# Round 0 sums its exponentials on VectorE, and v loads in three transfers per pair of heads

## The chip, the cores and the metric

One NeuronCore of a Trainium2 chip runs the whole program. The metric is device time in microseconds, the median of several runs. The engines named here are PE (TensorE, matrix products), DVE (VectorE), ACT (ScalarE), POOL (GpSimd) and SP (SyncE, which here only issues transfers).

## The reference

The program is an attention with capped scores, followed by a gated feed-forward block. There are 4 batch elements, 12 heads, 448 tokens and 64 features per head; the block has 768 inputs and 1536 inner features.

```python
def _attn_ref(q, k, v, cap):                       # q, k, v: (4, 12, 448, 64)
    scores = 1.0 / np.sqrt(64) * np.matmul(q, k.transpose(0, 1, 3, 2))
    scores = cap * np.tanh(scores / cap)
    attn = np.exp(scores - np.max(scores, axis=-1, keepdims=True))
    attn = attn / (np.sum(attn, axis=-1, keepdims=True) + 1e-09)
    return np.matmul(attn, v)

def _moe_ref(x, w_gate, w_val, w_out, rms_g):      # x: (1792, 768)
    xn = x / np.sqrt(np.mean(x * x, axis=-1, keepdims=True) + 1e-06) * rms_g
    g = xn @ w_gate                                # (768, 1536)
    return g * (1.0 / (1.0 + np.exp(-g))) * (xn @ w_val) @ w_out
```

The weights w_gate, w_val and w_out arrive as 64-bit floats.

## The kernel before

**Attention.** A round (`duo`, L397) handles two pairs of heads, a and b, so four heads; there are three rounds per batch element, twelve in all. Pair p of batch element b has the slot 6b + p, and slots take turns in two raw buffers (`raw0`, `raw1`), four transposed buffers (`qk0` to `qk3`) and four v buffers (`v0` to `v3`). Each pair loads q and k in eight transfers (`load_qk`, L365) and v in four (`load_v`, L377); DVE transposes raw into qk (`turn_qk`, L387).

A round has seven units. Each of the first six takes 128 keys of one pair: score products on PE into a wide bank, a tanh and an exp on ACT (128 x 896 elements each) into one of four buffers `e`, and the product with v on PE. The seventh unit takes the last 64 keys of both pairs. The sum of the exponentials over the keys is made in one of two ways. In rounds 0 to 7 PE multiplies every `e` by a matrix of ones into bank 6, after units 1, 3, 5 and 6. In rounds 8 to 11 (`SUM_FIRST`, L392) DVE first adds the six wide `e` of each pair, and PE then sums over partitions once. At the end of a round DVE transposes bank 6, inverts it, transposes that and scales the products in their banks into `xT`; ACT squares `xT`.

**Between attention and block** (`xconv`, L495) PE sums the squares over all heads into bank 6, DVE transposes that (`sumsq<-bank`), makes the inverse root, and scales six tiles of `xT`; ACT and DVE split each into two 16-bit parts, `xhl`.

**Block.** `ffn1` (L531) is 24 groups of 18 products of 128 x 448 columns per batch element, `out_proj` (L550) the second product. The weights are turned from 64-bit to 32-bit floats by DVE (`to_f32`, L284) and split into 16-bit parts by ACT and DVE: w_gate and w_val of batch 0 in `conv_gv` (L312), w_out in `conv_out` and `split_out`. Their staging buffers hold four pairs of tiles of 768 KB (four loads lead, L601; later ones wait for a buffer).

**Order.** Every operation is put into a list with a due time; `Plan.schedule` (L82) goes through the engines with assumed costs and takes, of the operations that are ready, the one due first. The result is a fixed order on each engine, and each engine works in that order. The due times of the block hang on `F0`, `L0`, `L1` (L253): batch 0's block is due from F0 on. Attention of batch 0 is due from 14 on, 2.15 per unit, and that of batch 1 from 70 on.

Of the kernel before, what the change touches and what calls it, by code (L numbers as in the profile page):

```python
# [10 lines left out]
F32 = mybir.dt.float32  # L11
# [7 lines left out]
P = 128  # L19
B, H, S, D = 4, 12, 448, 64  # L20
NPAIR = H // 2
NDUO = H // 4
# [108 lines left out]
def capped_attention__then__swiglu_ffn(  # L131
# [20 lines left out]
    V, A, G, T, SP = nc.vector, nc.scalar, nc.gpsimd, nc.tensor, nc.sync  # L152
# [9 lines left out]
    def free(ap):  # L162
        n = 1
        for x in ap.shape[1:]:
            n *= x
        return n

    def op(e, name, due, dst, *args, cost=None, **kw):
        reads = [x for x in (*args, *kw.values()) if isinstance(x, bass.AP)]
        writes = [dst]  # L170
        if "accum_out" in kw:
            writes.append(kw["accum_out"])
            reads = [x for x in reads if x is not kw["accum_out"]]
        n = free(dst) / 1000
        if cost is None:
            if e is A:
                cost = 0.2 + n * 0.92 + (0.19 if "accum_out" in kw else 0.0)
            elif e is V:
                quick = name in ("tensor_scalar", "tensor_copy", "tensor_single_scalar")
                quick = quick and all(x.space != PSUM for x in reads)  # L180
                cost = 0.16 + n * (0.54 if quick else 1.07)
            else:
                cost = 0.25 + n * 2.3
        plan.add(str(e.engine), cost, due, lambda: getattr(e, name)(dst, *args, **kw), writes, reads)  # L184
# [10 lines left out]
    def dma(due, dst, src, e=None):  # L195
        size = free(dst) * dst.shape[0] * mybir.dt.size(dst.dtype)
        q = e or SP
        plan.add("SP" if q is SP else str(q.engine), 0.52, due, lambda: q.dma_start(dst, src), [dst], [src], moved=size)  # L198
# [23 lines left out]
    cu = const.tile([P, DM], F32, name="cu")  # L222
# [3 lines left out]
    hT = const.tile([P, 2, NF, S], F16, name="hT")  # L226
# [23 lines left out]
    OUT_STAGE = (4, 5, 6, 7, 4, 5, 7, 4, 6, 5, 7, 6)  # L250


    F0, L0, L1 = 82.0, 178.0, 165.0  # L253
    start_of = [F0, F0 + L0, F0 + L0 + L1, F0 + L0 + 2 * L1]
    length = [L0, L1, L1, 124.0]
    ATT = ((70.0, 3.0), (135.0, 5.0), (250.0, 5.0))
# [4 lines left out]
    def att_due(b, d, step):  # L261

        n = 7 * d + step
        if b == 0:
            return 14.0 + 2.15 * n
        s, step = ATT[b - 1]
        return s + n * step
# [91 lines left out]
    def slot(b, p):  # L359
        return b * NPAIR + p  # L360

    def x_slot(b, p):
        return slot(b, p) % (NPAIR + 2)
# [13 lines left out]
    def load_v(b, p, due):  # L377

        t = v_t[slot(b, p) % 4]
        for hh in range(2):  # L380
            src = v[b, 2 * p + hh]
            dma(due, t[:, 3 * hh : 3 * hh + 3], src[0:384].rearrange("(c j) d -> j c d", c=3))
            dma(due, t[HALF[(hh + p) % 2], 6], src[384:S])

    HALF = (slice(0, 64), slice(64, 128))

    def turn_qk(b, p, due):  # L387
        raw, t = raws[slot(b, p) % 2], qk_t[slot(b, p) % 4]
        op(V, "transpose", due, t, raw)

    units = [0]
    SUM_FIRST = 8  # L392
    old_w = wo_all[:, 8 * DM : 10 * DM]
    acc_wide = old_w[:, 0 : 2 * S].rearrange("p (h s) -> p h s", h=2)
    acc = [[acc_wide[:, 0], acc_wide[:, 1]], [old_w[:, 2 * S : 3 * S], cu[:, 0:S]]]

    def duo(b, d):  # L397
        pa, pb = 2 * d, 2 * d + 1
        for p in (pa, pb):
            due = att_due(b, d, 0.5 * (p - pa))  # L400
            load_qk(b, p, due - 20)
            load_v(b, p, due - 12)
            turn_qk(b, p, due - 6)
        total = bank[6][:, 0:S]
        pv = [bank[i][:, 0:S] for i in ((4, 5) if b == 0 else (0, 1))]
        vt = [v_t[slot(b, p) % 4] for p in (pa, pb)]
        qk = [qk_t[slot(b, p) % 4] for p in (pa, pb)]
        es = {}
        for n in range(7):
            due = att_due(b, d, n)  # L410
            wide = pair[units[0] % 2 if b == 0 else 1]
            e = es[n] = e_t[units[0] % 4]
            units[0] += 1
            x, c = n % 2, n // 2
            if n < 6:
                mm(due, 0.9, *[
                    (wide[:, hh, 0:S], qk[x][HALF[hh], 1, c * P : (c + 1) * P], qk[x][HALF[hh], 0], True, True)
                    for hh in range(2)
                ])
            else:  # L420
                mm(due, 0.9, *[
                    (wide[HALF[(hh + x) % 2], x, 0:S], qk[x][HALF[hh], 1, 384:S], qk[x][HALF[hh], 0], True, True)
                    for x in range(2) for hh in range(2)
                ])
            op(A, "activation", due, e, wide[:, :, 0:S], AF.Tanh, scale=sc_t)
            op(A, "activation", due, e, e, AF.Exp, scale=capt)
            if n < 6:
                mm(due + 3, 0.85, *[
                    (pv[x][HALF[hh]], vt[x][:, 3 * hh + c], e[:, hh], c == 0, False) for hh in range(2)
                ])  # L430
            else:
                mm(due + 3, 0.85, *[
                    (pv[x][HALF[hh]], vt[x][HALF[(hh + x) % 2], 6], e[HALF[(hh + x) % 2], x], False, True)
                    for x in range(2) for hh in range(2)
                ])
            if NDUO * b + d >= SUM_FIRST:
                if n in (2, 3, 4, 5):
                    old = es[x] if n < 4 else None
                    if x == 0:
                        op(V, "tensor_add", due + 3, acc_wide, acc_wide if old is None else old, e)  # L440
                    else:
                        for hh in range(2):
                            op(V, "tensor_add", due + 3, acc[1][hh], acc[1][hh] if old is None else old[:, hh], e[:, hh])
                elif n == 6:
                    for y in range(2):
                        for hh in range(2):
                            h = HALF[(hh + y) % 2]
                            op(V, "tensor_add", due + 3, acc[y][hh][h], acc[y][hh][h], e[h, y])
                    mm(due + 4, 0.9, *[
                        (total[32 * (2 * hh + y) : 32 * (2 * hh + y) + 32], ones[:, 0:32], acc[y][hh], True, True)  # L450
                        for y in range(2) for hh in range(2)
                    ])
                continue
            if x == 1:
                mm(due + 4, 0.85, *[
                    (total[32 * (2 * hh + y) : 32 * (2 * hh + y) + 32], ones[:, 0:32], es[n - 1 + y][:, hh], c == 0, False)
                    for y in range(2) for hh in range(2)
                ])
            if n == 6:
                mm(due + 4, 0.85, *[  # L460
                    (
                        total[32 * (2 * hh + y) : 32 * (2 * hh + y) + 32],
                        ones[HALF[(hh + y) % 2], 0:32], e[HALF[(hh + y) % 2], y], False, True,
                    )
                    for y in range(2) for hh in range(2)
                ])
        due = att_due(b, d, 7) + 3
        xp = x_slot(b, pa)
        tmp = xT[:, xp]
        op(V, "transpose", due, tmp, total)  # L470
        first = tmp.rearrange("p (n i) -> p n i", i=32)[:, :, 0]
        op(V, "reciprocal", due, inv_t, first.unsqueeze(1).to_broadcast([P, 2, R14]), cost=0.3)
        for x in range(2):
            inv = inv_t[:, x]
            for hh in range(2):
                r = 64 * hh + 32 * x
                o = 64 * hh + 32 * (1 - x)
                op(V, "reciprocal", due, inv[o : o + 32], first[r : r + 32], cost=0.25)
        op(V, "transpose", due, dn_t, inv_t.unsqueeze(3).to_broadcast([P, 2, R14, 32]))
        both = xT[:, xp : xp + 2]  # L480
        if b == 0:
            for x in range(2):
                op(V, "tensor_mul", due, xT[:, xp + x], pv[x], dn_t[:, x])
        else:
            op(V, "tensor_mul", due, both, pair[0][:, :, 0:S], dn_t)
        if d == 0:
            op(A, "activation", due + 1, sumsq, both, AF.Square)
        else:
            op(A, "activation", due + 1, dn_t, both, AF.Square)
            if d < NDUO - 1:  # L490
                op(V, "tensor_add", due + 1, sumsq, sumsq, dn_t)
# [107 lines left out]
    for d in range(NDUO):  # L599
        duo(0, d)  # L600
# [51 lines left out]
```

## Time and profile before

| What | us |
|---|---|
| median of 3 runs (lowest, highest) | 731.34 (730.57, 732.25) |
| the profiled execution | 731.7 |
| its span, first to last instruction | 729.9 |
| PE busy in the span | 702.6 (96%) |
| DVE, ACT busy | 374.3, 331.3 |

The profile is one execution; 1.8 us of its time lie outside its span. Times below are from the start of the span. PE's busy time is the union of its products, so the rest, 27.3 us, is time in which PE had none.

### The profile page before, as it was taken

The numbers are of one execution on the slowest core, as the hardware profiler recorded it, in microseconds if no ns is written. First come the engines' busy times: TensorE is split into PE (matmuls) and PEld (weight loads), VectorE is DVE, ScalarE is ACT, GpSimd is POOL, SyncE is SP. The second block draws the span as 40 slices with busy tenths as digits, with TensorE's granted clock in tenths as the row PEclk, the third lists the DMA queues.
The fourth block names the chain that finished last, engine by engine and source line by source line (L and its number), as shares of the span: only waits on it lengthen the run. The fifth ranks groups of instructions, "written<-read, shape, count | busy, mean of one in ns | idle before, by whom it ended". The sixth has DMA issues, their size and how long they took to land.

```text
span 729.9 us, 9854 instructions
## 1 busy us (share of the span) xinstructions
PE 702.6 (96%) x3956; PEld 315.8 (43%) x3956; DVE 374.3 (51%) x606; ACT 331.3 (45%) x450; POOL 12.9 (2%) x18
## 2 busy tenths in 40 slices
PE   5987799999999899999999999999999999999998
PEld 1222233333443244443455553345555655555564
DVE  1667788888889894625223219762222162222211
ACT  5888777878568883344511105721111121111100
POOL 0001000100000000000000000000000000000000
PEclk9999899999999989999999999999999999999999
DMA  8895686845644514400000010000000100000010
GB/s 178 177 230 102 151 221 170 201 126 169 180 142 152 111 24 90 86 13 22 4 1 1 1 33 12 22 12 1 1 0 1 33 34 12 1 1 0 6 39 33
DMA packets 137741, 50.98 MB, mean 70 GB/s; under 512 B 114144, under 2 KB 136160, under 8 KB 137696
## 3 DMA queue, kind: packets, MB, share of 16 engines
q1 hardware_dynamic: 133984, 49.90, 27.0%
q10 hardware_dynamic: 3712, 0.46, 0.4%
q8 instruction: 31, 0.51, 0.3%
q14 instruction: 14, 0.11, 0.1%
HBM read 44.83 MB, written 5.51 MB: 69 GB/s over the span
## 4 chain that ended last, share of the span: by engine, by line
PE 86%; DMA 4%; DVE 4%; SPq 4%; ACT 1%; issue 1%; DVEq 0%
PE bank L191 71%; PE banks L191 15%; SPq L198 4%; DMA raw<-in_q_dram 2%; DVE wslot L184 1%; DVE cu L184 1%; DVE wo_all L184 1%; DMA wo_all<-in_moe_w_val_dram 1%; DMA osb_t<-in_moe_w_val_dram 1%; DMA osb_t<-in_moe_w_gate_dram 1%; ACT e L184 1%; DMA raw<-in_k_dram 1%; DVE qk L184 0%; ACT osb_t L184 0%; DVE xT L184 0%
## 5 line engine op out<-in xcount | busy, mean ns | idle before, releaser
L191 PE MATMUL bank<-xhl,wslot 128*128 128x448 f16 x1728 | 336.1, 353 | 0.5 <-DVE t L184 0.5
L191 PEld LDWEIGHTS <-wslot 128*128 128x128 f16 x1728 | 165.3, 98 | 183.9 <-issue 33.6
L184 DVE SCALAR_TENSOR_TENSOR t<-t,bank 128x448 f32<-128x448 f32 x96 | 59.5, 620 | 161.7 <-ACT t L184 83.5
L191 PEld LDWEIGHTS <-hT 128*128 128x128 f16 (+1 forms) x1152 | 97.5, 101 | 85.9 <-issue 28.8
L191 PE MATMUL bank<-wo_all,hT 128*128 128x384 f16 (+1 forms) x768 | 126.5, 327 | 0.0
L184 ACT ACTIVATE e<-banks,sc_t 128x896 f32<-128x896 f32 x84 | 84.0, 1001 | 45.3 <-PE banks L191 43.9
L191 PE MATMUL banks<-qk 64*128 64x448 f32 (+1 forms) x384 | 87.7, 597 | 14.8 <-DVE qk L184 10.5
L184 ACT ACTIVATE e<-e,capt 128x896 f32<-128x896 f32 x84 | 87.5, 1041 | 2.5
L184 ACT ACTIVATE hT<-t 128x448 f16<-128x448 f32 x48 | 27.6, 574 | 121.1 <-DVE t L184 121.1
L184 ACT ACTIVATE t<-bank,hs 128x448 f32<-128x448 f32 x48 | 30.4, 633 | 94.9 <-PE bank L191 94.8
L191 PE MATMUL bank<-osb_t,hT 128*128 128x384 f16 (+1 forms) x384 | 72.2, 337 | 0.0
L184 ACT ACTIVATE wo_all<-bank,sm 128x384 f32<-128x384 f32 x28 | 16.2, 580 | 107.5 <-PE bank L191 107.5
L184 DVE SCALAR_TENSOR_TENSOR wo_all<-bank,sm,wo_all 128x384 f32<-128x384 f32 x28 | 17.2, 614 | 92.0 <-PE bank L191 87.7
L191 PE MATMUL banks<-e,v 128*64 128x448 f32 (+1 forms) x288 | 60.2, 567 | 0.8 <-ACT e L184 0.8
L191 PEld LDWEIGHTS banks<-qk 64*128 64x128 f32 (+1 forms) x384 | 25.5, 177 | 63.1 <-issue 27.7
L184 DVE SCALAR_TENSOR_TENSOR hT<-hT,t 128x448 f16<-128x448 f16 x48 | 29.8, 622 | 26.3 <-ACT hT L184 26.2
L191 PE MATMUL bank<-e,ones 128*32 128x448 f32 (+1 forms) x256 | 31.7, 571 | 4.9 <-DVE sumsq L184 4.9
L184 DVE STREAM_TRANSPOSE qk<-raw 128x896 f32<-128x896 f32 x24 | 26.2, 1102 | 18.5 <-DMA raw<-in_q_dram 12.1
L191 PEld LDWEIGHTS banks<-e,v 128*64 128x64 f32 (+1 forms) x288 | 13.5, 135 | 29.7 <-issue 19.4
L184 DVE TENSOR_TENSOR wo_all<-wo_all,e 64x448 f32<-64x448 f32 (+2 forms) x20 | 13.9, 712 | 14.1 <-ACT e L184 14.0
L191 PE MATMUL bank<-e,v 128*64 128x448 f32 (+1 forms) x96 | 19.4, 559 | 1.2 <-ACT e L184 0.8
L184 DVE SCALAR_TENSOR_TENSOR wslot<-wo_all,sw,wslot 128x768 f16<-128x768 f32 x18 | 17.9, 1012 | 2.0 <-ACT wslot L184 1.9
(82 smaller groups left out, 367.5 us busy)
## 6 DMA issues: line engine op xcount, KB each, us to landing
wo_all<-in_moe_w_gate_dram SPq DMA_DIRECT2D x9, 768.0 KB, 4.9
wo_all<-in_moe_w_val_dram SPq DMA_DIRECT2D x9, 768.0 KB, 6.7
raw<-in_k_dram SPq DMA_DIRECT2D x96, 56.0 KB, 2.5
raw<-in_q_dram SPq DMA_DIRECT2D x88, 56.0 KB, 2.4
v<-in_v_dram SPq DMA_DIRECT2D x48, 96.0 KB, 2.5
wo_all<-in_moe_w_out_dram SPq DMA_DIRECT2D x6, 768.0 KB, 4.5
osb_t<-in_moe_w_out_dram SPq DMA_DIRECT2D x6, 768.0 KB, 4.5
out_dram<-wo_all SPq DMA_DIRECT2D x24, 192.0 KB, 1.9
```

The costliest lines, as they stand in the source:

```text
L184: plan.add(str(e.engine), cost, due, lambda: getattr(e, name)(dst, *args, **kw), writes, reads)
L191: T.matmul(dst, l, r, start=start, stop=stop)
L198: plan.add("SP" if q is SP else str(q.engine), 0.52, due, lambda: q.dma_start(dst, src), [dst], [src], moved=size)
```

## The change

Three edits. Round 0 now sums its exponentials like rounds 8 to 11: DVE adds, into 32-bit words laid over `hT` (which the block first writes after attention of batch 0), and PE sums once. There both pairs have a wide accumulator, so their additions are of 128 x 896. The v rows of both heads of a pair, keys 0 to 383, come in one transfer in which partition j holds the three keys 3j, 3j+1, 3j+2 of each head, 768 bytes that lie together; the last 64 keys stay one transfer per head. So that scores and v agree on the keys of a block, the score products take every third key, `c:384:3`, as weights, in all twelve rounds. And F0 is 76 instead of 82.

```diff
-    F0, L0, L1 = 82.0, 178.0, 165.0
+    F0, L0, L1 = 76.0, 178.0, 165.0
...
         t = v_t[slot(b, p) % 4]
+        dma(
+            due,
+            t[:, 0:6].rearrange("j (h c) d -> j h (c d)", h=2),
+            v[b, 2 * p : 2 * p + 2, 0:384].rearrange("h (j c) d -> j h (c d)", c=3),
+        )
         for hh in range(2):
             src = v[b, 2 * p + hh]
-            dma(due, t[:, 3 * hh : 3 * hh + 3], src[0:384].rearrange("(c j) d -> j c d", c=3))
             dma(due, t[HALF[(hh + p) % 2], 6], src[384:S])
...
-    SUM_FIRST = 8
+
+    SUM_ROUNDS = (0, 8, 9, 10, 11)
     old_w = wo_all[:, 8 * DM : 10 * DM]
...
+    hT_words = hT.bitcast(F32).rearrange("p a j s -> p (a j s)")
+    first_wide = [hT_words[:, 2 * S * i : 2 * S * (i + 1)].rearrange("p (h s) -> p h s", h=2) for i in range(2)]
+    first_acc = [[w[:, 0], w[:, 1]] for w in first_wide]
...
+        acc, acc_wide = (first_acc, first_wide) if b == 0 else (late_acc, [late_wide])
...
-                    (wide[:, hh, 0:S], qk[x][HALF[hh], 1, c * P : (c + 1) * P], qk[x][HALF[hh], 0], True, True)
+                    (wide[:, hh, 0:S], qk[x][HALF[hh], 1, c:384:3], qk[x][HALF[hh], 0], True, True)
...
-            if NDUO * b + d >= SUM_FIRST:
+            if NDUO * b + d in SUM_ROUNDS:
                 if n in (2, 3, 4, 5):
                     old = es[x] if n < 4 else None
-                    if x == 0:
-                        op(V, "tensor_add", due + 3, acc_wide, acc_wide if old is None else old, e)
+                    if x < len(acc_wide):
+                        op(V, "tensor_add", due + 3, acc_wide[x], acc_wide[x] if old is None else old, e)
```

Since due times and operations change, the fixed order changes on every engine. Three places of it follow.

DVE in rounds 0 and 1, the kernel before: from the first weight tile to the transpose of round 0's sums (`xT<-bank6`); qk2 and qk3 are the transposed pairs of round 1.

```order
L184 TENSOR_SCALAR wslot0_82<-wo_all_94 128x1536
L184 SCALAR_TENSOR_TENSOR wslot0_82<-wo_all_94,wslot0_82 128x1536
L184 STREAM_TRANSPOSE qk2_107<-raw0_103 128x896
L184 SCALAR_TENSOR_TENSOR wo_all_94<-wo_all_94,wslot0_82 128x1536
L184 STREAM_TRANSPOSE qk3_108<-raw1_104 128x896
L184 STREAM_TRANSPOSE xT_97<-bank6_65 128x448
```

The same place of the changed kernel.

```order
L184 TENSOR_TENSOR hT_100<-e0_109,e2_111 128x896
L184 TENSOR_TENSOR hT_100<-e1_110,e3_112 128x896
L184 TENSOR_SCALAR wslot0_82<-wo_all_94 128x1536
L184 TENSOR_TENSOR hT_100<-hT_100,e0_109 128x896
L184 STREAM_TRANSPOSE qk2_107<-raw0_103 128x896
L184 TENSOR_TENSOR hT_100<-hT_100,e1_110 128x896
L184 STREAM_TRANSPOSE qk3_108<-raw1_104 128x896
L184 TENSOR_TENSOR hT_100<-hT_100,e2_111 64x448 x4
L184 SCALAR_TENSOR_TENSOR wslot0_82<-wo_all_94,wslot0_82 128x1536
L184 STREAM_TRANSPOSE xT_97<-bank6_65 128x448
```

The eight additions stand in between; the last four come behind the transpose of qk3, and one weight operation has moved behind them.

SP in the kernel before, from the second gate tile (`osb_t`) to the loads of slot 4. The order also lists, for every transfer from the tenth on, a wait for the transfer eight places before it.

```order
L198 DMA osb_t_95<-in_moe_w_gate_dram 128x6x256
L198 DMA v2_115<-in_v_dram 128x3x64
L198 DMA v2_115<-in_v_dram 64x64
L198 DMA v2_115<-in_v_dram 128x3x64
L198 DMA v2_115<-in_v_dram 64x64
L198 DMA v3_116<-in_v_dram 128x3x64
L198 DMA v3_116<-in_v_dram 64x64
L198 DMA v3_116<-in_v_dram 128x3x64
L198 DMA v3_116<-in_v_dram 64x64
L198 DMA osb_t_95<-in_moe_w_val_dram 128x6x256
L198 DMA raw0_103<-in_k_dram 32x14x32 x4
L198 DMA raw0_103<-in_q_dram 32x14x32 x4
```

The same place of the changed kernel.

```order
L198 DMA osb_t_95<-in_moe_w_gate_dram 128x6x256
L198 DMA v2_115<-in_v_dram 128x2x192
L198 DMA v2_115<-in_v_dram 64x64 x2
L198 DMA v3_116<-in_v_dram 128x2x192
L198 DMA v3_116<-in_v_dram 64x64 x2
L198 DMA osb_t_95<-in_moe_w_val_dram 128x6x256
L198 DMA raw0_103<-in_k_dram 32x14x32 x4
L198 DMA raw0_103<-in_q_dram 32x14x32 x4
```

Six transfers instead of eight lie between the gate tile and the val tile, so the val tile is the seventh after the gate tile and not the ninth.

DVE before the statistic of batch 0, the kernel before (qk0 is slot 8, `sumsq<-bank6` the transposed sum of squares).

```order
L184 SCALAR_TENSOR_TENSOR wslot3_85<-wo_all_94,wslot3_85 128x1536
L184 RECIPROCAL sw_75<-ma_74 128x2
L184 STREAM_TRANSPOSE qk0_105<-raw0_103 128x896
L184 SCALAR_TENSOR_TENSOR wo_all_94<-wo_all_94,wslot3_85 128x1536
L184 STREAM_TRANSPOSE sumsq_99<-bank6_65 128x448
```

The same place of the changed kernel.

```order
L184 TENSOR_SCALAR mx_73<-mx_73 128x2 x2
L184 SCALAR_TENSOR_TENSOR wo_all_94<-wo_all_94,wslot3_85 128x1536
L184 RECIPROCAL sw_75<-ma_74 128x2
L184 STREAM_TRANSPOSE qk0_105<-raw0_103 128x896
L184 STREAM_TRANSPOSE sumsq_99<-bank6_65 128x448
```

The transpose of slot 8 still stands ahead of the statistic, and the weight operation that stood between them now stands ahead of both.

## Rows read from the trace of the kernel before

**Rows 1.** The page, part 1: busy us, share of the span, instructions.

```profile
PE 702.6 (96%) x3956; PEld 315.8 (43%) x3956; DVE 374.3 (51%) x606; ACT 331.3 (45%) x450; POOL 12.9 (2%) x18
```

**Rows 2.** Windows: length, busy time (instructions) by engine, granted clock, DMA share, GB/s.

```profile
40.00:50.00 10.00, 7.84 (x52) 2.20 (x52) 5.02 (x10) 7.72 (x9) 0.00 (x0) 1.00 0.96 265
80.00:90.00 10.00, 10.00 (x43) 2.79 (x44) 9.59 (x25) 6.52 (x10) 0.00 (x0) 0.70 0.49 86
180.00:260.00 80.00, 75.91 (x397) 27.87 (x396) 72.88 (x118) 59.72 (x86) 1.65 (x3) 0.96 0.52 148
```

**Rows 3.** Timeline of PE: start, duration, operation, idle time before and releaser.

```profile
12.81 1.02 PE L191 MATMUL banks<-qk 64*128 64x448 f32 x4
13.76 0.96 PE L191 MATMUL bank<-e,ones 128*32 128x448 f32 x8
14.65 1.02 PE L191 MATMUL banks<-qk 64*128 64x448 f32 x4
...
73.06 1.02 PE L191 MATMUL banks<-qk 64*128 64x448 f32 x4
...
79.89 1.72 PE L191 MATMUL bank<-e,ones 128*32 128x448 f32 x8 [4.89 <-DVE sumsq L184]
...
87.33 3.20 PE L191 MATMUL bank<-xhl,wslot 128*128 128x448 f16 x16
...
253.69 1.86 PE L191 MATMUL banks<-qk 64*128 64x448 f32 x4 [1.41 <-ACT e L184]
255.49 4.83 PE L191 MATMUL bank<-osb_t,hT 128*64 128x384 f16 x20
```

**Rows 4.** Timeline of DVE around the statistic of batch 0.

```profile
76.52 1.11 DVE L184 STREAM_TRANSPOSE qk<-raw 128x896 f32<-128x896 f32 x1 [3.83 <-DMA raw<-in_q_dram]
77.56 1.72 DVE L184 SCALAR_TENSOR_TENSOR wo_all<-wo_all,wslot 128x1536 int32<-128x1536 int32 x1
79.19 0.64 DVE L184 STREAM_TRANSPOSE sumsq<-bank 128x448 f32<-128x448 f32 x1
...
82.84 3.67 DVE L184 SCALAR_TENSOR_TENSOR xT<-xT,ck,sumsq 128x448 f32<-128x448 f32 x6
```

**Rows 5.** The chain that ended last: start, duration, what (SPq: an issue).

```profile
22.75 4.92 DMA osb_t<-in_moe_w_gate_dram
27.68 0.95 SPq L198
...
71.50 4.75 DMA raw<-in_q_dram
```

**Rows 6.** Timeline of SP's issues, with the time they took.

```profile
23.27 5.36 SPq L198 DMA_DIRECT2D v<-in_v_dram  x8
28.67 0.59 SPq L198 DMA_DIRECT2D osb_t<-in_moe_w_val_dram  x1
...
39.85 6.60 SPq L198 DMA_DIRECT2D v<-in_v_dram  x8
46.51 0.58 SPq L198 DMA_DIRECT2D wo_all<-in_moe_w_gate_dram  x1
...
61.53 5.74 SPq L198 DMA_DIRECT2D v<-in_v_dram  x10
67.37 2.00 SPq L198 DMA_DIRECT2D raw<-in_k_dram  x4
...
71.03 0.42 SPq L198 DMA_DIRECT2D wo_all<-in_moe_w_gate_dram  x1
```

**Rows 7.** Timeline of ACT: the last exp of batch 0's third round.

```profile
58.40 1.04 ACT L184 ACTIVATE e<-e,capt 128x896 f32<-128x896 f32 x1
```

**Rows 8.** Groups by form: count, busy us, mean ns, idle us before.

```profile
L184 DVE TENSOR_TENSOR wo_all<-e,e 128x896 f32<-128x896 f32 x4 | 4.3, 1083 | 1.8 <-ACT e L184 1.8
L184 DVE TENSOR_TENSOR wo_all<-wo_all,e 64x448 f32<-64x448 f32 x12 | 7.1, 615 | 2.1 <-ACT e L184 1.9
L191 PEld LDWEIGHTS banks<-qk 64*128 64x128 f32 x288 | 23.0, 193 | 56.7 <-issue 22.3 <-ACT e L184 18.7 <-DVE qk L184 9.0
```

More of the change, by code (lines that the diff above doesn't have):

```diff
@@ L391, in capped_attention__then__swiglu_ffn @@
     units = [0]
-    SUM_FIRST = 8
+    SUM_ROUNDS = (0, 8, 9, 10, 11)
     old_w = wo_all[:, 8 * DM : 10 * DM]
-    acc_wide = old_w[:, 0 : 2 * S].rearrange("p (h s) -> p h s", h=2)
-    acc = [[acc_wide[:, 0], acc_wide[:, 1]], [old_w[:, 2 * S : 3 * S], cu[:, 0:S]]]
+    late_wide = old_w[:, 0 : 2 * S].rearrange("p (h s) -> p h s", h=2)
+    late_acc = [[late_wide[:, 0], late_wide[:, 1]], [old_w[:, 2 * S : 3 * S], cu[:, 0:S]]]
+    hT_words = hT.bitcast(F32).rearrange("p a j s -> p (a j s)")
+    first_wide = [hT_words[:, 2 * S * i : 2 * S * (i + 1)].rearrange("p (h s) -> p h s", h=2) for i in range(2)]
+    first_acc = [[w[:, 0], w[:, 1]] for w in first_wide]
     def duo(b, d):
```

## Prediction

> **What bounds the kernel now.** I read the page's busy times first. PE is busy for 702.6 of 729.9 us, so the end is PE's work plus 27.3 us in which it has none [rows 1]. The second view, PE's timeline, shows where those are. The block starts with the product from `xhl` at 87.33 [rows 3]; behind it the only window with idle time before the last product is 180 to 260, with 80 − 75.91 = 4.1 us [rows 2], the largest gap there at 253.69; the output product starts at 255.49. The rest lies before 87.33, but for some 3.5 us after the last product. So two questions decide: when does the block start, and does the stretch from there to the output product still fill?
>
> Back from 87.33. The longest gap, 4.89 us, ends at 79.89, released by DVE's `sumsq`: the transposed sum of squares frees bank 6, in which attention of batch 1 waits to sum [rows 3]. The sums themselves were done when PE went on to the next score group at 73.06. DVE's timeline shows what came between: it waited 3.83 us for a load of q, transposed that (slot 8) at 76.52, did one weight operation of 1.72 us, and only then, at 79.19, the transpose of the sums [rows 4]. The load was issued at 71.50 and took 4.75 us; a weight tile had been issued just ahead of it, at 71.03 [rows 5, 6], and such a tile takes about as long (4.92). So what sets the block's start is SP's list of issues and the transfers on it, not the arithmetic. After the gap the granted clock averaged 0.70 from 80 to 90 [rows 2], between its levels of 1.2 and 2.4 GHz, and a group of ones took 1.72 instead of 0.96 us [rows 3].
>
> How SP comes to be late is seen in the chain and in SP's timeline. The second gate tile took from 22.75 to 27.67, and the last of the eight v transfers behind it began to issue at 27.68 [rows 5]. In the order each transfer waits for the one eight places before it, and here the trace shows such a wait end. So the val tile went out at 28.67. The next eight v issues took 6.60 us, though eight issues of 0.55 make 4.4: two weight tiles were ahead of them [rows 6].
>
> **The change part by part.**
>
> *Fewer v issues.* One of four per pair goes, 24 in all. I walk SP's list with 0.55 us an issue and the waits of the changed order.
> - The first two pairs of v save 1.2 us; the loads of slot 3 then end 1.3 earlier, at about 23.5.
> - The second val tile has six v transfers between it and its gate tile, so its wait is no longer for that tile. It goes out at 28.67 − 1.25 − 1.1 − 1.1 = 25.2, that is 3.4 earlier (issues before it, issues between, the wait).
> - The loads of slots 4 and 5 follow 3.3 earlier. The gate tile after the next v's goes out at 40.2 instead of 46.51: 3.3, two issues (1.1) and most of the 2.2 us of waiting in the 6.60.
> - Its data cannot be as early as that. From 40 to 50 the DMA engines were busy at a share of 0.96 [rows 2], and the v rows are the same bytes in pieces three times as long. I let 4.3 us of the 6.3 stand, and slot 7 goes out that much earlier.
> - Then eight v issues instead of ten (the 5.74 at 61.53 [rows 6]) give 1.1 to 1.6 more. The load of q for slot 8 still goes behind a weight tile, at about 65.6 instead of 71.50, and lands at about 70.4 instead of 76.25: 5.9 earlier. With none of the waits gone, only 8 x 0.55 = 4.4 would be; with no limit by the DMA engines about 8.
>
> *DVE before the statistic.* In the changed order the weight operation of 1.72 us stands ahead of slot 8's transpose, so it runs while DVE waits. The transpose of the sums then starts at 70.4 + 1.1 = 71.5, 7.7 earlier than 79.19. This needs the sums by then. ACT ended the third round's last exp at 59.44 [rows 7]; with the loads of rounds 1 and 2 earlier I put that at 57, `xT` at 64.7, the last square at 66.4 and PE's sums at 68.1. If rounds 1 and 2 gain nothing, the sums are ready at 73.06 as before, and the statistic moves by 6.1 instead of 7.7.
>
> *The additions.* Round 0 gets four of 1.08 and four of 0.615 us [rows 8], 6.8 us of DVE as single durations. DVE is idle between its items in this stretch, but these stand in a bad place: the last four wait behind the transpose of qk3, a load that I expect at 23.5, and one weight operation (like the 1.72 of [rows 4]) now follows them ahead of the transpose of round 0's sums. I get that at 28.6, some 2.1 later than before. Behind it are the scaling into `xT`, the release of PE's v banks, and ACT's square. I expect ACT to stand about 1.2 us there, and later to win it back, since it waited for loads. At worst the delay goes through, 2.3 us with ACT's stand, to the statistic: sums at 75.4, a gain of 3.8.
>
> *PE's part of round 0.* Three groups of ones of 0.89 us each (13.76 to 14.65 [rows 3]) go, 2.7 us of PE work. They lie where PE waits for loads and ACT, so I count nothing for them beside the earlier start. One group of the four stays.
>
> *Every third key as weights.* 72 groups of scores load their weights with a step of 12 bytes (288 loads, four a group). No row of this trace has such a load. Now a load of 128 columns takes 193 ns [rows 8], and a group with it lasts 0.95 us (12.81 to 13.76) against 0.89 for a group of ones, whose loads are of 32 columns [rows 3]: 96 columns show as 0.06 us. From below I see no way for a wider step to be quicker: nothing. From above, if one load's whole 0.193 us were added to each group, 13.9 us. I take nothing, by the nearest rows: most of a load lies beside the products ahead of it, and loads that took twice as long would show 0.08 a group, 5.8 us in all.
>
> The Trainium skill speaks against this edit (SBUF — State Buffer, Door 1: The DMA port swizzle): memory is read in lines of 16 bytes and needs at least two accesses to a line for full speed, while the same place calls steps of up to four fp32 free; a step of 12 bytes meets a line 1.3 times. No run here shows it yet. By its first half the loads slow down and the rival on the weights below gains; by its second half the sum stays.
>
> *F0 and the order after it.* Up to the output product, attention of batch 1 and 2 now has three score groups fewer in the order, 2.85 us of PE work that moves behind. Before that product PE had gaps and DVE was 91% busy (72.88 of 80 us [rows 2]); DVE's list up to the scales of w_out has four scalings of `xT` less (0.60 each by starts, from 82.84 [rows 4]) and one transpose (1.1) more, 1.3 us less. If DVE sets the start of the output product, the stretch shrinks by 1.3 and the rest grows by 2.85: a loss of 1.5. If PE does, the group at 253.69 that waited for ACT simply goes, and nothing is lost. I take a loss of 0.7.
>
> **Sum.** 731.7 (the profiled execution) − 7.7 + 0.7 = 724.7. That execution lies 0.36 above the median of the runs shown, so 724.3.
>
> **Rivals.**
> - *The transfers set the pace, not the issues.* For it: the share of 0.96. Against it: the chain runs through issues, and from 60 on there is room. Then only shorter pieces count; I put slot 8 at 2.5 us earlier, and with the weight operation (1.6) and the loss of 0.7 that is 3.4: about 728.
> - *More than I take.* If slot 8 lands by 68.3, the sums at 68.1 set the statistic, 9.7 earlier; without the long gap the clock stays up, and PE's seven groups before the block, which took 87.33 − 79.89 = 7.4 us, take 6 (up to 1.5 more). About 721.
> - *DVE's weight work sets the output product whatever the block's start.* For it: 91% busy. Against it: DVE's gaps there are waits for PE and ACT, which move along. Then 255.49 stays and the moved groups come on top: 731 to 734, no change or a little slower.
> - *Strided weights slow PE.* One mechanism, in every score group of all rounds, most of them where PE has no gap. At 0.1 us a group the gain is gone (7.2); at 0.193 it is 724.3 + 13.9 = 738, slower than before. It decides from 0.12 us a group. Against it: the loads lie mostly beside products.
>
> **How the numbers follow.** Forecast 0.46 (own range 722 to 727); transfers 0.16; more 0.20; DVE's weight work 0.08; strided weights 0.10, of which half ends slower than before. I call faster or slower what differs by more than 0.2%, about what runs of this kernel can tell: below 729.9 or above 732.8. Faster gets the first three and a share of the last, 0.84; same 0.08; slower 0.08. The range of 8 in 10 leaves out some of either end: 720 to 731.
>
> **What would show it.** Right: the first product from `xhl` at 79 to 80; the transpose of the sums straight behind that of slot 8, at 71 to 72; the second val tile issued near 25; no gap of PE over 3 us after 10 and a granted clock near 1.00 from 70 to 90; the output product near 248; a load of 64x128 still at 193 ns and score groups at 0.95. Wrong: val tile early but slot 8 after 73 (transfers); `xT` of round 0 after 34 and never made up (additions); the output product still at 255 (DVE); score groups over 1.0 us (weights).

## The result and the profile after

The changed kernel took 725.35 us (median of 4 runs, 724.65 to 726.34), the kernel before beside it 731.19 (4 runs). The ratio is 0.9918, with 95% certainty between 0.9902 and 0.9934. The forecast was 724.3, in a range of 720 to 731. All ratios here leave out one execution of an experiment below (e4) that took 2490 us.

The profiled execution took 724.9 us with a span of 723.1, so 6.8 less than before. The page first, the answer to [rows 1]:

```profile
PE 703.5 (97%) x3932; PEld 324.6 (45%) x3932; DVE 379.7 (53%) x614; ACT 332.7 (46%) x450; POOL 13.2 (2%) x18
```

PE is busy 0.9 us longer, though round 0 gave up 2.7 us of its work; its idle time fell from 27.3 to 723.1 − 703.5 = 19.6. The windows answer to [rows 2], with two more:

```profile
40.00:50.00 10.00, 6.59 (x40) 2.27 (x34) 9.36 (x15) 7.32 (x10) 0.34 (x1) 0.93 1.07 325
50.00:60.00 10.00, 10.00 (x54) 2.52 (x50) 9.11 (x14) 8.44 (x10) 2.43 (x2) 0.90 0.65 112
70.00:80.00 10.00, 8.27 (x35) 1.96 (x34) 7.81 (x20) 8.53 (x13) 1.39 (x1) 0.83 0.86 200
80.00:90.00 10.00, 9.84 (x53) 4.48 (x50) 9.31 (x20) 9.11 (x17) 0.61 (x2) 1.00 0.49 130
180.00:260.00 80.00, 77.08 (x445) 30.53 (x444) 73.98 (x119) 62.14 (x92) 1.64 (x3) 1.00 0.48 135
```

The granted clock fell at other places: it is 1.00 from 80 to 90 and from 180 to 260, where it was 0.70 and 0.96, and below 1 from 40 to 60 (0.93, 0.90) and from 70 to 80 (0.83; before 0.96). PE's timeline, the answer to [rows 3]:

```profile
48.72 3.26 PE L191 MATMUL bank<-e,v 128*64 128x448 f32 x8 [2.90 <-DVE xT L184]
...
69.35 1.77 PE L191 MATMUL bank<-dn,ones 128*128 128x448 f32 x4
71.05 1.09 PE L191 MATMUL banks<-qk 64*128 64x448 f32 x4
72.07 0.97 PE L191 MATMUL banks<-e,v 128*64 128x448 f32 x4
74.78 0.96 PE L191 MATMUL bank<-e,ones 128*32 128x448 f32 x8 [1.73 <-DVE sumsq L184]
...
81.08 0.74 PE L191 MATMUL bank<-xhl,wslot 128*128 128x448 f16 x3
...
245.38 0.79 PE L191 MATMUL bank<-osb_t,hT 128*64 128x384 f16 x5
246.09 0.96 PE L191 MATMUL bank<-e,ones 64*32 64x448 f32 x8
246.98 1.99 PE L191 MATMUL bank<-osb_t,hT 128*64 128x384 f16 x15
```

The long gap of 4.89 is now 1.73. The block starts at 81.08 (−6.25). From there to the output product it takes 164.30 us instead of 168.16 (−3.86), and behind that 477.72 instead of 474.41 (+3.31): together −6.8. The first twenty products of the output take 0.79 + 1.99 us; before they took 4.83. DVE, the answer to [rows 4], with round 1 ahead:

```profile
40.39 1.11 DVE L184 STREAM_TRANSPOSE qk<-raw 128x896 f32<-128x896 f32 x1 [3.31 <-DMA raw<-in_q_dram]
41.43 1.72 DVE L184 SCALAR_TENSOR_TENSOR wslot<-osb_t,wslot 128x1536 int32<-128x1536 int32 x1
43.18 1.76 DVE L184 SCALAR_TENSOR_TENSOR osb_t<-osb_t,wslot 128x1536 int32<-128x1536 int32 x1
44.85 0.64 DVE L184 STREAM_TRANSPOSE xT<-bank 128x448 f32<-128x448 f32 x1
...
73.08 1.11 DVE L184 STREAM_TRANSPOSE qk<-raw 128x896 f32<-128x896 f32 x1 [1.49 <-DMA raw<-in_k_dram]
74.11 0.61 DVE L184 STREAM_TRANSPOSE sumsq<-bank 128x448 f32<-128x448 f32 x1
```

The transpose of the sums stands straight behind that of slot 8, as the order said, but at 74.11 and not at 71.5. SP's issues show why, the answer to [rows 5, 6] (`gcol` is the one small transfer behind the gate tile at 42.59; the loads at 54.64 are the first of slot 7):

```profile
25.63 0.59 SPq L198 DMA_DIRECT2D osb_t<-in_moe_w_val_dram  x1
...
38.67 3.88 SPq L198 DMA_DIRECT2D v<-in_v_dram  x6
42.59 0.59 SPq L198 DMA_DIRECT2D wo_all<-in_moe_w_gate_dram  x1
45.57 0.37 SPq L198 DMA_DIRECT2D gcol<-in_moe_rms_g_dram  x1
...
54.64 1.99 SPq L198 DMA_DIRECT2D raw<-in_k_dram  x4
...
58.81 4.61 SPq L198 DMA_DIRECT2D v<-in_v_dram  x8
...
65.54 1.52 SPq L198 DMA_DIRECT2D raw<-in_q_dram  x3
67.16 0.42 SPq L198 DMA_DIRECT2D wo_all<-in_moe_w_gate_dram  x1
67.63 0.54 SPq L198 DMA_DIRECT2D raw<-in_q_dram  x1
```

Slot 7 in the kernel before:

```profile
57.37 1.99 SPq L198 DMA_DIRECT2D raw<-in_k_dram  x4
```

The last transfer of slot 8's q still goes out behind a weight tile, at 67.63 instead of 71.50. It took 5.17 us and landed at 72.80; the transposition follows 0.28 later, as it did before (76.25, 76.52), although its row names a load of k.

The score groups, the answer to the load in [rows 8]: the load of 64x128 went from 193 to 256 ns, and a group lasts 1.02 us by starts (71.05 to 72.07) instead of 0.95.

```profile
L191 PEld LDWEIGHTS banks<-qk 64*128 64x128 f32 x288 | 31.6, 256 | 47.7 <-issue 21.5 <-ACT e L184 13.1 <-DVE qk L184 10.6
```

So the sum came out within 1.1 us. It stays open whether its terms did: the step was taken at nothing and shows, F0 was charged with a loss, and the block starts 1.5 us later than forecast.

### The profile page after: what moved, and what is told of

It is laid out like the page before. It is cut to its first block, busy times and chain, and to the rows that moved or that the text cites. A ratio compares the mean times of both kernels' runs of the same rounds, so it can differ in the third digit from the quotient of the medians.

```text
span 723.1 us, 9790 instructions
## 1 busy us (share of the span) xinstructions
PE 703.5 (97%) x3932; PEld 324.6 (45%) x3932; DVE 379.7 (53%) x614; ACT 332.7 (46%) x450; POOL 13.2 (2%) x18
## 4 chain that ended last, share of the span: by engine, by line
PE 88%; SPq 4%; DVE 4%; DMA 3%; ACT 1%; issue 1%; DVEq 0%
PE bank L191 73%; PE banks L191 14%; SPq L198 4%; DMA raw<-in_k_dram 1%; DMA raw<-in_q_dram 1%; DVE xT L184 1%; DMA v<-in_v_dram 1%; ACT e L184 1%; DVE wo_all L184 0%; DVE cu L184 0%; DVE inv L184 0%; DVE dn L184 0%; DVE qk L184 0%; DVE rs_t L184 0%; ACT osb_t L184 0%
## 5 line engine op out<-in xcount | busy, mean ns | idle before, releaser
L191 PE MATMUL banks<-qk 64*128 64x448 f32 (+1 forms) x384 | 91.7, 619 | 10.4 <-DVE qk L184 7.8
L191 PE MATMUL bank<-osb_t,hT 128*128 128x384 f16 (+1 forms) x384 | 70.2, 327 | 0.0
L191 PEld LDWEIGHTS banks<-qk 64*128 64x128 f32 (+1 forms) x384 | 34.1, 225 | 54.5 <-issue 24.2
L191 PE MATMUL bank<-e,ones 128*32 128x448 f32 (+1 forms) x224 | 26.7, 551 | 1.7 <-DVE sumsq L184 1.7
L191 PE MATMUL bank<-e,v 128*64 128x448 f32 (+1 forms) x96 | 21.4, 608 | 2.9 <-DVE xT L184 2.9
```

What stands on the lines that cost most here:

```text
L191: T.matmul(dst, l, r, start=start, stop=stop)
```

## The experiments

Each was timed beside runs of the kernel before on the same chip (medians 730.0 for e1 to e4, 731.05 for e5 to e8, 730.26 for e9 to e12). Ratios are to those, and brackets are 95% intervals; microseconds are the ratio times 731.

**e1, the step alone.** The kernel before with

```diff
-                    (wide[:, hh, 0:S], qk[x][HALF[hh], 1, c * P : (c + 1) * P], qk[x][HALF[hh], 0], True, True)
+                    (wide[:, hh, 0:S], qk[x][HALF[hh], 1, c:384:3], qk[x][HALF[hh], 0], True, True)
...
-            dma(due, t[:, 3 * hh : 3 * hh + 3], src[0:384].rearrange("(c j) d -> j c d", c=3))
+            dma(due, t[:, 3 * hh : 3 * hh + 3], src[0:384].rearrange("(j c) d -> j c d", c=3))
```

> The kernel before with every third key as weights; v keeps its four transfers per pair (keys 3j to 3j+2 together, 768 bytes), F0 and the sums stay, and the fixed order on every engine is the one of before. Theory A (the step costs TensorE time): a load of 64x128 takes 256 ns instead of 193, a group of scores 1.02 us instead of 0.95; the 48 groups behind the start of the block lie where TensorE has no gap, 48 x 0.07 = 3.4 us, and with those ahead of it up to 72 x 0.07 = 5.0: 734.5 to 736.2. Rival B (the longer load is hidden, what the changed kernel lost it lost elsewhere): loads longer, groups 0.95, time 731. Rival C (longer pieces of v make the transfers faster and so the loads of q and k earlier): the first product from xhl before 86, time under 731 plus A's cost.

Ratio 1.0032 [1.0020, 1.0043], 2.3 us slower. The load and slot 8's transposition (start, duration, wait):

```profile
L191 PEld LDWEIGHTS banks<-qk 64*128 64x128 f32 x288 | 31.7, 257 | 54.4 <-issue 20.8 <-ACT e L184 16.9 <-DVE qk L184 9.0
```

```profile
78.61 1.11 DVE L184 STREAM_TRANSPOSE qk<-raw 128x896 f32<-128x896 f32 x1 [4.10 <-DMA raw<-in_q_dram]
```

With the order unchanged, PE's busy time rose by 5.6 us (702.6 to 708.2), and its idle time fell by 2.1 (27.3 to 25.2): theory A in kind, but 2.3 us [1.5, 3.1] is under the 3.4 that it had as its least. Longer pieces of v hasten nothing here: slot 8's transposition still waits 4.10 us for q and starts later than before (76.52), so C falls. The step slows PE in rounds 0 to 2 as well, so the clearer sign is SP's list. With longer pieces but as many transfers, from the second gate tile to its val tile takes 6.14 us (23.25 to 29.39), where it took 5.92 before and takes 4.06 in the changed kernel; and the eight v issues that took 6.60 us take no less:

```profile
40.94 6.88 SPq L198 DMA_DIRECT2D v<-in_v_dram  x8
```

**e2, contiguous keys by the transposition.** The changed kernel with raw and transposed halves swapped (k first) and

```diff
-        op(V, "transpose", due, t, raw)
+        flat, wide = (x.rearrange("p h s -> p (h s)") for x in (raw, t))
+        op(V, "transpose", due, wide[:, 0:384].rearrange("p (c j) -> p j c", c=3), flat[:, 0:384])
+        op(V, "transpose", due, wide[:, 384:], flat[:, 384:])
...
-                    (wide[:, hh, 0:S], qk[x][HALF[hh], 1, c:384:3], qk[x][HALF[hh], 0], True, True)
+                    (wide[:, hh, 0:S], qk[x][HALF[hh], 0, c * P : (c + 1) * P], qk[x][HALF[hh], 1], True, True)
```

> The changed kernel, with the transposition writing every third key of k side by side, so that the weights of the scores have no step; v keeps its three transfers. VectorE transposes each pair in two instructions (384 columns of k in the new places, 512 columns of the rest). Theory A: loads back at 193 ns, groups at 0.95 us, 48 x 0.07 = 3.4 us less behind the start of the block, and up to 1.6 more ahead of it: 720.3 to 722. Rival B (the longer load is hidden): 725.3. Rival C (VectorE writes with a step of 512 bytes at a lower rate, the 384 columns take 1 us and more instead of some 0.5): the start of the block moves back by up to 2 us and the time is 725 or above.

Ratio 1.0018 [1.0003, 1.0033]: the whole gain gone. By form:

```profile
L191 PEld LDWEIGHTS banks<-qk 64*128 64x128 f32 x288 | 23.3, 194 | 53.4 <-issue 20.2 <-ACT e L184 20.2 <-DVE qk L184 10.5
...
L184 DVE STREAM_TRANSPOSE qk<-raw 128x384 f32<-128x384 f32 x24 | 20.4, 852 | 9.5 <-DMA raw<-in_k_dram 5.2 <-PE banks L191 4.2
L184 DVE STREAM_TRANSPOSE qk<-raw 128x512 f32<-128x512 f32 x24 | 16.4, 689 | 4.8 <-DMA raw<-in_q_dram 4.6
```

```profile
180.00:260.00 80.00, 72.00 (x412) 28.72 (x412) 75.11 (x123) 60.05 (x90) 2.43 (x3) 1.00 0.48 133
```

PE's busy time fell by 5.2 us, as A says (703.5 to 698.3). But a transposition now takes 0.852 + 0.689 = 1.54 us instead of 1.10, and PE's idle time rose from 19.6 to 29.5; from 180 to 260 it is 8.0 instead of 2.9, while DVE is busy for 75.1. Rival C in the time, though 852 ns is under the 1 us that it named, and the block's start did not move back (81.25 for 81.08). The order shifted too (fewer score groups stand ahead of the output product), so not all of the idle time is the transposition's.

**e3, v and the step; e4, the sums.** e3 is the changed kernel with

```diff
-    F0, L0, L1 = 76.0, 178.0, 165.0
+    F0, L0, L1 = 82.0, 178.0, 165.0
...
-    SUM_ROUNDS = (0, 8, 9, 10, 11)
+    SUM_ROUNDS = (8, 9, 10, 11)
```

and e4 the changed kernel with the first of these, and with v's four transfers and contiguous keys as before.

> The kernel before with v in three transfers and every third key as weights; F0 82 and the sums of round 0 on TensorE. Theory A (the earlier start of the block comes from the issues of v on SyncE, by way of the loads of q and k): the second val tile goes out near 25.5, the first product from xhl at 81 to 83 instead of 87.3, time 726 to 728. Rival B (it comes from the sums of round 0 leaving TensorE): the first product from xhl at 86 or later, and with the cost of the step 733 or more.

> The kernel before with round 0's sums on VectorE alone: v in four transfers, contiguous keys, F0 82. Its fixed order on SyncE is that of before up to slot 7, but on VectorE the transposition of slot 8 has moved behind the statistic, with a weight operation of 1.7 us in its place. Theory A (the loads on SyncE and the place of slot 8's transposition set the statistic): loads of rounds 1 and 2 as before, sums of squares ready near 73 to 75, transposed at 75 to 77 instead of 79.2, first product from xhl at 83 to 85, time 727 to 729. Rival B (the sums on VectorE bring the earlier start by themselves): sums ready at 71 and the block at 81, time 725 or less. Rival C (the additions stand in VectorE's way): sums later than 75.5, time 731 or more.

e3: 0.9930 [0.9917, 0.9942], 5.1 us faster, with the val tile at 25.87. e4: 0.9983 [0.9974, 0.9992], 1.2 us. The statistic and the first product of the block in e3:

```profile
70.67 0.64 DVE L184 STREAM_TRANSPOSE sumsq<-bank 128x448 f32<-128x448 f32 x1
```

```profile
77.42 0.36 PE L191 MATMUL bank<-xhl,wslot 128*128 128x448 f16 x1
```

v with its step gives nearly the whole gain of the changed kernel; A holds for e3, and the block starts 4 us earlier than A thought, in an order in which slot 8's transposition stands behind the statistic. So e3 prices the edit of v together with that place. e4 lies between A and C: the statistic at 77.11, `xhl` at 82.09. There slot 8 stands behind too, and a load sets the statistic all the same: the weight operation ahead of it waits for a val tile.

```profile
76.23 0.96 DVE L184 TENSOR_SCALAR wslot<-wo_all 128x1536 int32<-128x1536 int32 x1 [3.05 <-DMA wo_all<-in_moe_w_val_dram]
77.11 0.64 DVE L184 STREAM_TRANSPOSE sumsq<-bank 128x448 f32<-128x448 f32 x1
```

**e5, the step only where it pays.** e3 with

```diff
+    STEP_ROUNDS = 4
...
+        keys = [slice(c, 384, 3) if NDUO * b + d < STEP_ROUNDS else slice(c * P, (c + 1) * P) for c in range(3)]
```

and v in four transfers of contiguous keys from slot 8 on.

> The kernel of e3 (three transfers of v, F0 82, round 0's sums on TensorE), but every third key and three transfers only in rounds 0 to 3; rounds 4 to 11 use contiguous keys and four transfers. Its order on TensorE and VectorE is that of e3. Theory A (the step costs 0.07 us a group, and after round 3 nothing waits for the issues of v): start of the block as in e3 (77.4), 8 rounds x 6 groups x 0.07 = 3.4 us less than e3: 722 where e3 had 725.3. Rival B (what e3 gained came from the transfers of all rounds): slower than e3 or the same. Rival C (the longer load of later rounds lies where something else sets the pace): 725.

Ratio 0.9875 [0.9854, 0.9896], 721.9 us: 4.0 us under e3, where 3.4 was worked out. A. It saves 8 of the 24 issues, those of slots 0 to 7, and nothing is seen to be lost by the other 16.

**e6, slot 8's transposition held back.** The changed kernel; the planner is told that this operation reads the statistic.

```diff
+        behind = [rs_t[:, 1]] if slot(b, p) in (8,) else []
-        op(V, "transpose", due, t, raw)
+        op(V, "transpose", due, t, raw, behind=behind)
```

> The changed kernel with one thing held back in VectorE's fixed order: the transposition of slot 8 stands behind the statistic and the split into xhl. Theory A (the load of slot 8 sets the statistic, in the changed kernel still): the transpose of the sums at 71.3 instead of 74.1, right behind the sums, first product from xhl at 78 to 79 instead of 81.1, and as TensorE is full behind it 722.3 to 723.5. Rival B (the start is given back, since round 4's scores now come later and ACT has less time for them before the output product): start earlier, but the output product still near 245 and the time 725. Rival C: the statistic does not move, since the sums themselves come later in the new order.

Ratio 0.9899 [0.9879, 0.9918].

```profile
70.92 0.64 DVE L184 STREAM_TRANSPOSE sumsq<-bank 128x448 f32<-128x448 f32 x1
```

```profile
76.65 0.74 PE L191 MATMUL bank<-xhl,wslot 128*128 128x448 f16 x3
...
244.51 2.70 PE L191 MATMUL bank<-osb_t,hT 128*64 128x384 f16 x20
```

The statistic moved by 3.2 us, so in the changed kernel slot 8's load did set it. The block starts 4.4 us earlier, the output product only 0.9, and the time is 1.4 lower by the ratios, whose intervals overlap. A for the start (76.65, where it had 78 to 79); the time, 723.6, lies between A and B.

**e7, F0 and v; e8, F0 and the sums.** e7 is the changed kernel with the second part of e3's diff alone; e8 is it with v's four transfers and contiguous keys as before.

> The changed kernel with round 0's sums back on TensorE; F0 76 and the three transfers of v stay. Theory A (v's issues carry the gain, F0 and the sums nearly cancel): 725 to 726, start of the block near 77 as in e3. Rival B (F0 gains by itself): 723 or less. Rival C (F0 costs, the sums make up for it): 727 or more.

> The changed kernel without the edit of v: four transfers, contiguous keys; F0 76 and round 0's sums on VectorE stay. Theory A (v's issues carry the gain): start of the block at 82 to 85 as in e4, time 728 to 730, a little under the kernel before, though TensorE is spared the 5 us of the step. Rival B (F0 with the sums gains as much as v): 726 or less.

e7: 0.9899 [0.9877, 0.9921]; e8: 0.9956 [0.9939, 0.9973]. e7, 723.6, lies between A and B, nearer to B; e8, 727.8, between its A and B. With the sums of round 0 back on PE the changed kernel is faster, if anything (the intervals overlap). The statistic of e8:

```profile
76.49 0.64 DVE L184 STREAM_TRANSPOSE sumsq<-bank 128x448 f32<-128x448 f32 x1
```

DVE and PE of e7 at the place of the gap of 2.90 above:

```profile
33.00 0.95 DVE L184 TENSOR_SCALAR wslot<-osb_t 128x1536 int32<-128x1536 int32 x1
...
40.95 1.11 DVE L184 STREAM_TRANSPOSE qk<-raw 128x896 f32<-128x896 f32 x1 [2.40 <-DMA raw<-in_q_dram]
43.42 0.37 DVE L184 TENSOR_SCALAR mx<-mx 128x2 int32<-128x2 int32 x2 [1.35 <-ACT wslot L184]
45.33 0.65 DVE L184 STREAM_TRANSPOSE xT<-bank 128x448 f32<-128x448 f32 x1 [1.53 <-PE bank L191]
```

```profile
48.40 1.00 PE L191 MATMUL bank<-e,ones 128*32 128x448 f32 x8
49.33 2.48 PE L191 MATMUL bank<-e,v 128*64 128x448 f32 x12
```

Here the weight operations are done before the load lands, the transpose of round 1's sums waits for PE instead, and PE reaches the products with v at 49.33 without a gap. In the changed kernel it reached that place 2.9 us too soon, waited until 48.72, and the clock read 0.93 from 40 to 50 and 0.90 from 50 to 60. The work that PE gave up in round 0 became a wait.

**e9, e5 with F0; e10, F0 alone; e11, F0 at 70; e12, v and the sums.** e9 is e7 with e5's edit, e10 the kernel before with `F0 = 76`, e11 is e9 with `F0 = 70`, e12 the changed kernel with `F0 = 82`.

> The kernel of e7 (F0 76, three transfers of v, round 0's sums on TensorE) with the step and the three transfers only in rounds 0 to 3, as in e5. Theory A (the gains add: fewer issues early, F0, no step later): e7 less 8 x 6 x 0.07 = 3.4 us, so 720 beside a kernel before of 731 (ratio 0.985 to 0.986). Rival B (without the step TensorE reaches the waits before the output product sooner and loses there what it gained): 722 to 723.5.

> The kernel before with F0 76 alone. Theory A (F0 gains by itself: it takes three score groups and a group of ones out of the stretch before the output product, where TensorE waited for ACT and the granted clock fell): product start of the output near 250, about 2 us less than before, ratio 0.997. Rival B (my prediction: the groups only move behind, a loss of 0.7): ratio 1.001. Start of the block as before, 87.3, by both.

> The kernel of e9 with F0 70. Its order has three more score groups and four more products with v behind the start of the output product. Theory A (what stands in that stretch waits for ACT, so less of it is better): 1 to 2 us less than e9. Rival B (VectorE's work on w_out then sets the start of the output product and TensorE waits there): 1 us or more above e9. Rival C: within 1 us of e9.

> The changed kernel with F0 82. Theory A (the edit of v gives 5 us alone, the sums of round 0 give 1 where they stand alone and cost 1.4 beside v, F0 gives 2): 727 to 728 beside a kernel before of 731. Rival B (the edits simply add): 731 - 5.1 - 1.2 = 724.7. In either case slot 8's transposition still stands ahead of the statistic.

e9: 0.9857 [0.9842, 0.9872], 720.5 us, where A had 720. It beats both kernels; its PE is idle for 718.8 − 702.4 = 16.4 us. e12: 0.9969 [0.9953, 0.9985], 728.7 us, near A (727 to 728) and far from B.

e10: 0.9957 [0.9943, 0.9972], 3.1 us faster; my prediction's B falls. Its windows and its output product:

```profile
80.00:90.00 10.00, 9.62 (x51) 3.42 (x44) 9.72 (x22) 7.41 (x12) 0.00 (x0) 0.89 0.41 74
...
180.00:260.00 80.00, 76.76 (x442) 28.84 (x441) 74.40 (x119) 62.51 (x91) 1.63 (x3) 1.00 0.49 134
```

```profile
248.42 0.78 PE L191 MATMUL bank<-osb_t,hT 128*64 128x384 f16 x5
```

The groups moved behind the output product as forecast. PE's idle time in the window fell only from 4.1 to 3.2 us, but the clock is 1.00 there instead of 0.96, and 0.89 instead of 0.70 from 80 to 90. Before the block nothing is won by that, since it is 0.83 from 60 to 70, where it was 1.00. That the start of the block stays, as both theories said, was wrong: it moved to 85.19.

e11: 0.9983 [0.9967, 0.9999], 9.2 us above e9; B in size. PE's idle time from 180 to 260 is 8.1 us where e9 has 1.9, and the largest piece of it is a wait for DVE's weights, though at a product from `xhl` and not at the output product that B named:

```profile
213.74 4.78 PE L191 MATMUL bank<-xhl,wslot 128*128 128x448 f16 x16 [2.89 <-DVE wslot L184]
```

That is a single point: F0 is not "less is better", and where its best value lies was not tried.

The three edits in all combinations, from one profile each (span, PE busy, idle) and the timed ratio; S is the sums of round 0, V the edit of v with its step. The column "slot 8" says whether its transposition stands ahead of the statistic on DVE or behind it:

| kernel | slot 8 | ratio | span | PE busy | idle | first `xhl` | output product |
|---|---|---|---|---|---|---|---|
| before | ahead | 1 | 729.9 | 702.6 | 27.3 | 87.33 | 255.49 |
| S (e4) | behind | 0.9983 | 727.4 | 699.2 | 28.2 | 82.09 | 253.08 |
| F0 (e10) | ahead | 0.9957 | 724.6 | 701.4 | 23.2 | 85.19 | 248.42 |
| V (e3) | behind | 0.9930 | 723.3 | 704.3 | 19.0 | 77.42 | 246.90 |
| F0, S (e8) | behind | 0.9956 | 724.1 | 697.3 | 26.8 | 82.42 | 247.68 |
| V, S (e12) | ahead | 0.9969 | 725.4 | 702.9 | 22.5 | 79.59 | 249.18 |
| V, F0 (e7) | behind | 0.9899 | 721.7 | 703.3 | 18.4 | 77.15 | 243.46 |
| all three | ahead | 0.9918 | 723.1 | 703.5 | 19.6 | 81.08 | 245.38 |
| all three (e6) | behind | 0.9899 | 721.7 | 701.4 | 20.3 | 76.65 | 244.51 |

Read in pairs, without e6: F0 gains 0.27 to 0.51% in each of four pairs (2.0 to 3.7 us; beside V alone the intervals overlap), and V 0.14 to 0.70% (they overlap beside S alone). S gains 0.17% alone, nothing beside F0, and seems to cost 0.39% beside V (0.19% beside both, overlapping).

But V and S also move slot 8: either of them puts its transposition behind the statistic, both together leave it ahead. So these pairs price an edit together with that place, and e6 parts the two. With slot 8 behind in both, all three edits (e6) and V with F0 (e7) have the same ratio, 0.9899, each within some 0.2%: the sums then neither gain nor cost that can be seen. And with slot 8 behind, F0 and S in both, V takes the statistic from 76.49 to 70.92 and the ratio from 0.9956 to 0.9899 (e8 to e6), 4.2 us: this is what V, its step included, is worth by itself.

## Why the prediction came out, point by point

- *Bound and place: right.* What the edit of v removes is PE's wait for the statistic. In the changed kernel slot 8's load sets that (e6), and with slot 8 out of the way, but without V, another load (e4). It is fewer issues and not longer pieces: with the pieces alone (e1) the val tile comes no sooner behind its gate tile, and the next eight v issues take 6.88 us, where six take 3.88 in the changed kernel.
- *The val tile: right*, 25.63 for 25.2, 3.0 us earlier. Of that 1.9 was lost over the loads of slots 4 and 5: the tile took 6.7 us to land instead of 5.1, and the v issues behind these loads, begun at 39.85 before, began at 38.67. These six took 3.88 us where eight took 6.60, which gave 2.7 back. The gate tile behind them went out 3.9 us earlier, where I had worked out 6.3.
- *Slot 8: the shift was too large.* I let 4.3 of the 6.3 stand for slot 7, and it went out 2.7 earlier (54.64 for 57.37). The two v issues fewer behind it gave 1.1, as forecast. What failed is the step from the gate tile to slot 7: in the changed order `gcol` is the transfer eight places behind the val tile issued at 38.03. That tile landed at 45.55, only 0.4 earlier than before, while the DMA engines' share from 40 to 50 was 1.07, and `gcol` went out at 45.57. The wait that the v issues no longer had stood one transfer further on. So the last piece of q went out 3.9 us earlier instead of 5.9, and its transposition began at 73.08, 3.4 earlier. With the weight operation out of the way that makes 5.1 for the statistic, not 7.7. It is the term "4.3 stand", and with it "5.9 earlier", that was mis-sized.
- *The sums ready at 68.1: wrong.* They were ready at 71.05 (before 73.06). So even a load in time could have given little over 3 us more; e6 shows that limit at 70.92. (The rival that gains more put this limit 9.7 us earlier; that number follows from slot 8 landing by 68.3 and its transposition, not from the sums at 68.1.)
- *The additions: the place was seen, the price was not.* The transpose at 28.59 was forecast at 28.6. I let ACT win the delay back and counted nothing for PE's 2.7 us. That work became a wait: PE comes to round 1's products early and waits 2.90 us for `xT`. The kernels with S beside V are slower by 2.9 us (e12 against e3) and by 1.4 with F0 (all three against e7, intervals that overlap), but e6 against e7 shows no cost once slot 8 stands behind the statistic. That points to the place of slot 8's transposition, 4.4 us of the block's start in e6, and not to the sums themselves; the 1.4 us of time between e6 and the changed kernel lie within their intervals.
- *The step: the step of the argument that failed.* I took nothing, with 5.8 us as the value for loads that take twice as long. A load took 256 ns, a third longer, and a group 0.07 more: 5.0 us of PE work, of which 2.3 (e1) to 4.0 (e5 against e3, eight rounds) show in the time. Taking most of a load as hidden was reading too much into the 96 columns that showed as 0.06 us: that row compares groups of another kind, and 0.07 was inside the bounds I had kept. The Trainium skill (SBUF — State Buffer, Door 1: The DMA port swizzle) had the two halves named in the prediction. The loads here, 256 ns against 193, agree with the first, lines of 16 bytes that need two accesses each for full speed, and not with the second, steps up to four fp32 free.
- *F0: the sign was wrong.* I took a loss of 0.7 and the runs show a gain of 2.0 to 3.7 in four pairs. I had the group at 253.69 as a wait that "simply goes", and the clock of 0.96 from 180 to 260 in [rows 2], but gave the clock no price there. 0.04 of 80 us is 3.2 us of PE at full rate; the output's first twenty products (4.83 instead of 2.78 us) and the score group ahead of them (1.86 instead of 1.02) make 2.9 of it. This explains F0 where the clock was low, in the kernel before (0.96 in e4 too). It doesn't explain F0 beside V, where the clock of that window was at 1.00 without F0 (e3, then e12):

```profile
180.00:260.00 80.00, 76.82 (x437) 31.57 (x436) 72.77 (x118) 60.18 (x87) 2.79 (x3) 1.00 0.47 132
```

```profile
180.00:260.00 80.00, 74.89 (x415) 30.37 (x417) 73.58 (x120) 59.66 (x86) 2.40 (x3) 1.00 0.47 132
```

From e12 to the changed kernel PE's idle time in the window fell from 5.1 to 2.9 us; from e3 to e7 it hardly moved (3.2 to 3.0), and the gain of that pair isn't clear of noise.
- *Together.* In the changed kernel the block started 1.45 us later than forecast (81.08 for 87.33 − 7.7). Behind that, 48 groups with 0.07 us of step each make 3.4 us, an estimate, for which I had nothing. The net change behind the start was a gain of 0.55, so the rest, F0 and its order, gained some 3.9 where I had a loss of 0.7. The misses, 1.45 and 3.4 on one side and 4.6 on the other, nearly cancel, and the total was right by that luck. The bound and the first part of the chain were not luck: V without its step would be worth 4.2 + 2.3 = 6.5 us (e8 to e6, and e1), where I had 7.7. The chance of 0.10 for the weights was too low for a price that no row bounded tightly.

Of the signs listed, the val tile, the order of the two transposes and the lack of a gap over 3 us held. The block's start, the time of the statistic, the clock (0.83 from 70 to 80), the load of 64x128 and the score groups did not, and the output product came 2.6 us earlier than "near 248". Two signs of rivals showed: slot 8's transposition after 73 (by 0.08), which is the transfers' part in the losses above, and score groups over 1.0 us, the sign of the weights.

Left open: how much of the small differences between orders is the order itself. Every edit that changes a cost or a due time shuffles the fixed order on the engines. e6 took out one such place, slot 8's; others were not held still, so the pairs above price an edit together with its order.

## What to carry to other kernels

Price a layout by all its readers: fewer issues on SP brought the block forward, but the same choice put a step into 288 weight loads of PE. Using it only in the rounds where loads are waited for gave 9.1 us (e5), in all rounds 5.1 (e3). Work taken off an engine that waits anyway can turn into a longer wait, as the 2.90 us in round 1 did. Where two edits seem to spoil each other, look first at what the pair did to the fixed order: with one operation moved (e6) the apparent cost of the sums was gone. Where a window shows a granted clock below 1.00, work out what it costs before costing an edit that moves work into or out of that window.

## What the runs showed of the hardware

- A weight load of 128 fp32 columns with a step of 12 bytes takes 256 to 257 ns against 193 to 194 without one, in each of the kernels above where the rows are shown; a group of scores with four of them 1.02 us against 0.95.
- DVE's transposition of 384 columns that writes with a step of 512 bytes took 852 ns, more than that of 512 columns side by side (689).
- The same twenty output products took 4.83 us in the kernel before, behind gaps of 1.11 and 1.41 us, the last of them 1.8 us ahead, and 2.78 us in the changed kernel, where the last gap (0.83 us) ended 3.7 us ahead of them. The window of the former, in the kernel before, shows the lower level of the clock, 1.2 GHz (0.50):

```profile
255.00:260.00 5.00, 5.00 (x22) 1.14 (x20) 5.00 (x7) 5.00 (x7) 0.00 (x0) 0.50 0.20 46
```
